# Selective attention and a SwiGLU block on one core: loads of batch 0 and tile 0 in another order and on another queue, narrow score banks, and the first down product by halves

## The chip, the cores and the metric

One core of a Trainium2 chip runs the whole program. TensorE (PE) multiplies, VectorE (DVE), ScalarE (ACT) and GpSimd (POOL) do the rest, SyncE (SP) only issues transfers. The metric is device time in microseconds (us), lower is better, as the median of several runs.

## The reference

Eight batches of eight heads, 576 positions, head size 64, all float32. Causal attention with a bias from the running sum of `max(s, 0)`; its output, as 4608 tokens of 512, goes through a SwiGLU block of width 1536.

```python
scores = scale * np.matmul(q, k.transpose(0, 1, 3, 2))
cum = np.cumsum(np.maximum(s, 0.0), axis=-1)
bias = -(cum[:, :, :, None] - cum[:, :, None, :])
scores = np.where(causal, -1000000000.0, scores + np.minimum(bias, 0.0))
attn = softmax(scores)
x = (attn @ v).transpose(0, 2, 1, 3).reshape(4608, 512)
g = x @ w_gate
out = (g * sigmoid(g) * (x @ w_val)) @ w_out
```

## The kernel before

The order of all work is written out by hand: each engine runs its instructions in the order in which the program emits them, and semaphores hold one engine until another is done. So where a line stands decides what is queued behind it.

**Attention.** Heads are taken in groups of four (`hb`, 0 to 15), k and q of one group being one load each (`load_one`, 576 KB). Before their use they are cast to bfloat16 (`cast_one`, `cast_half`), turned so that the head's dimension lies across partitions, and put into `KQ[hb % 2]`. For groups 0 to 4 TensorE turns them (`pe_transpose`, then `pe_out` copies them out of PSUM, one copy for each pair of heads, `r`); from group 5 (`NPE`) on they go out to DRAM (`scratch`), come back by a DMA transpose (`transposes`) and are copied into place by DVE (`split`, held in the list `later` and emitted by `do_later`). Four more rows of `KQ` hold the bias: running sums and constants from the tile `HL`, sent there by four small transfers a group (`aug`). The product of the 68 used rows gives score and bias together, keys across partitions.

`score_piece(bh, ci)` makes the scores of head `bh` in four pieces: the four diagonal blocks (512 columns), two pieces of 512 columns below them, and the last diagonal block (64). In batch 0 (`pair`) two pieces share a PSUM tile two banks wide, and one exponential takes 1024 or 576 columns; later, each piece has its bank and its exponential. GpSimd then zeroes the upper triangles of the diagonal blocks (`affine_select`, L391 and L396). `av_piece` multiplies with V (`VT`, filled chunk by chunk by `cast_v`), with a column of ones that gives the sum; `av_out` divides. A pair of heads is then turned into `XT`, by TensorE for batches 0 and 1 (`x_pe`), later through DRAM.

**Feed-forward.** Tokens go in nine tiles of 512 (`tt`), which do not begin where batches do. `gate_value` makes 24 items a tile, gate and value products in turn, 12 column blocks (`ft`) of each; weights lie in halves `j` of 768 columns, loaded and cast by GpSimd's transfers (`w_load`). `down_plain` (tiles 0 and 1) multiplies back with `WO`, four blocks of 128 tokens one after the other; `down_seven` does it with seven products for eight in the rest.

**The order.** At the start, `first_batch` emits batch 0 head by head, with loads, casts and transposes between. A second set of eight one-bank PSUM buffers (`take` gives the one released longest ago, `give` hands it back) then takes the place of the first set. After that the main loop walks through the items of each tile; after every item `pump` emits as much attention of the next batch (`attn_items`) as the item's number says. For tile 0 it starts at item `n0`. Between score pieces, `side`, `side_v` and `PREP_AT` emit loads, casts and transposes at fixed places (head, piece). `hook` does so at items of tile 0.

**Queues.** Loads of k, q and V and the transposes are issued on SP; weights, most of `aug` and the stores on GpSimd, whose own work waits while it issues. V's tile has one buffer (`bufs=1`), so that a batch's V is loaded only when the last one's is cast. k and q have three buffers.

Of the kernel before, what the change touches and what calls it, by code (L numbers as in the profile page):

```python
# [19 lines left out]
def kernel(  # L20
# [18 lines left out]
    NCH = 5  # L39
# [67 lines left out]
    PTP = {0: first, "bufs": 8}  # L107

    with tc.manual_schedule():
# [3 lines left out]
        first_psum = ExitStack()  # L113
        psa = first_psum.enter_context(tc.tile_pool(name="psa", bufs=1, space=PSUM))
        bank = {}
        for i in range(2):
            bank["w", i] = psa.tile([128, 1024], FP32, name=f"wide{i}")
        for i in range(4):
            bank["s", i] = psa.tile([128, 512], FP32, name=f"one{i}")
        released = {key: i - 8 for i, key in enumerate(bank)}  # L120
# [3 lines left out]
        def take(kind="s"):  # L124
            b = min((x for x in bank if x[0] == kind), key=lambda x: released[x])
            assert released[b] < OPEN
            released[b] = OPEN
            return b
# [5 lines left out]
        def second_psum():  # L134
            assert all(x < OPEN for x in released.values())
            at_end = dict(released)
            first_psum.close()
            psb = ctx.enter_context(tc.tile_pool(name="psb", bufs=1, space=PSUM))
            bank.clear()
            released.clear()  # L140
            for i in range(8):
                bank["s", i] = psb.tile([128, 512], FP32, name=f"bank{i}")
                released["s", i] = at_end["w", i // 2] if i < 4 else at_end["s", i - 4]

# [6 lines left out]
        def load_one(hb, name, rs=(0, NR)):  # L151
            b, g = divmod(hb, 2)
            if rs[0] == 0:
                loaded[name, hb] = raw.tile([128, NR, J, D], FP32, tag="raw" + name, name="raw" + name)
            nc.sync.dma_start(
                loaded[name, hb][:, rs[0] : rs[1], :, :].rearrange("x r j d -> x r (j d)"),
                SRC[name][0][b, g * HB + 2 * rs[0] : g * HB + 2 * rs[1], :, :].rearrange(
                    "(r e) (p j) d -> (e p) r (j d)", e=2, j=J
                ),
            )  # L160
# [5 lines left out]
        def load_v(b, cs):  # L166
# [3 lines left out]
            for c in cs:  # L170
                n = 128 if c < 4 else TAIL
                nc.sync.dma_start(  # L172
# [13 lines left out]
        NEGS2 = -1.0058441162109375  # L186

# [22 lines left out]
        load_qk(1)  # L210
# [6 lines left out]
        make_identity(nc, ident)  # L217

# [10 lines left out]
        pads(0)  # L229
        init_vt(0)  # L230
        init_vt(1)
        nc.vector.memset(aug_rows(1, 0), 0.0)
        nc.gpsimd.memset(aug_rows(1, 1), 0.0)
# [114 lines left out]
        scs = {}  # L348

        def score_piece(bh, ci):  # L350
            hb, hh = divmod(bh, HB)
            pair = bh < H
            if ci == 0:
                pts[bh] = PTP[0].tile(
                [128, PTW], BF16, tag="pt", bufs=PTP["bufs"], name="pt"
            )
# [3 lines left out]
            if pair:  # L360
                if ci % 2 == 0:
                    bs = take("w")
                    scs[bh] = bs
                else:
                    bs = scs[bh]
                base = (512, 0, 0, 512)[ci]
            else:
                bs = take()
                base = 0
            o = base  # L370
            n = sum(hi - lo for _, lo, hi in CHUNKS[ci])
            sc = view(bs, 1024 if pair else 512)
            for (tj, lo, hi) in CHUNKS[ci]:
# [5 lines left out]
                    start=True,  # L379
                    stop=True,  # L380
                )
                o += w
            if not pair or ci % 2 == 1:
                if pair:
                    c0, W = ((576, 1024), (0, 576))[ci // 2]
                else:
                    c0, W = CHUNK_PT[ci], n
                nc.scalar.activation(pt[:, c0 : c0 + W], sc[:, 0:W], AF.Exp, scale=0.125)  # L388
                give(bs)
            if ci == (1 if pair else 0):  # L390
# [89 lines left out]

        def side(h, step, ci):
            bh = HB * h + step
            if bh == H + 3 and ci == 1:
                for c in range(5):
                    cast_v(1, c, nc.gpsimd)
            if h >= 3 and h + 3 < NHB and (step, ci) == (0, 1):
                load_qk(h + 3)
            hb = h + 1
            if NPE <= hb < NHB:
                late = hb == NPE  # L490
                if (step, ci) == (0, 1):
                    if late:
                        transposes(hb)
                    aug(hb, GP4)
                first = 1 if hb < NPE + 2 else 0
                if step in (first, first + 1) and ci == 1:
# [3 lines left out]
            if NPE <= hb < NHB:  # L500
                late = hb == NPE
                if (step, ci) == ((1, 1) if late else (0, 2)):
                    cast_one(hb, "k", nc.scalar)
                if (step, ci) == ((2, 1) if late else (1, 2)):
                    cast_one(hb, "q", nc.scalar)
                if (step, ci) == ((3, 1) if late else (2, 0)):
                    scratch(hb)
                if (step, ci) == (3, 3 if hb == NPE + 1 else 0) and not late:
# [5 lines left out]
            if 2 <= bn < B:  # L514
# [5 lines left out]

        V_AT = {(1, 0): 0, (2, 0): 1, (2, 2): 2, (3, 0): 3, (3, 2): 4}

        def side_v(h, step, ci):
            bn = h // 2 + 1
            if 2 <= bn < B and h % 2 == 1 and (step, ci) in V_AT:
                cast_v(bn, V_AT[step, ci], nc.scalar if bn > 2 else nc.gpsimd)

        def prep_one(hb, i):
# [3 lines left out]
            for r in range(2):  # L532
                pe_out(hb, nm, g, r, nc.scalar if nm == "k" else nc.vector)

        PREP_AT = {
            2: {(0, 3): 0, (1, 3): 1, (2, 1): 2, (2, 3): 3},
# [5 lines left out]
            H + 5: (H + 2, H + 3), H + 6: (H + 4, H + 5), H + 7: (H + 6,),  # L542
        }
        X_AT = {H + 3: (), H + 5: (H + 1,), H + 6: (H + 3,), H + 7: (H + 5,)}

        def attn_items():
            for kk in range(H, BH + 2):
                h, step = divmod(kk, HB)
                if kk < BH:
# [5 lines left out]
                    if step == 0 and 3 < h + 1 < NPE:  # L555
# [62 lines left out]

        def gate_value(tt, hps, sus):
            xt = XT[:, :, (tt % 3) * TT : (tt % 3 + 1) * TT]  # L620
            for ft in range(NFT):
                j, f0 = divmod(ft * 128, WCH)
                gbs = take()
                pg = view(gbs, TT)
                for c in range(4):
                    nc.tensor.matmul(  # L626
                        pg, WG[j][:, c, f0 : f0 + 128], xt[:, c, :],
                        start=(c == 0), stop=(c == 3),
                    )
# [8 lines left out]
                vbs = take()  # L638
                pv = view(vbs, TT)
                for c in range(4):  # L640
                    nc.tensor.matmul(  # L641
                        pv, WV[j][:, c, f0 : f0 + 128], xt[:, c, :],
                        start=(c == 0), stop=(c == 3),
                    )
# [19 lines left out]
        def down_plain(tt, hps):  # L664
            for ts_ in range(4):
                ybs = take()
                py = view(ybs, DM)
                half, c0 = divmod(ts_ * 128, HT)
                for ft in range(NFT):
                    nc.tensor.matmul(  # L670
                        py, hps[ft // 2][:, 2 * (ft % 2) + half, c0 : c0 + 128],
                        WO[ft // WKO][:, ft % WKO, :],
                        start=(ft == 0), stop=(ft == NFT - 1),
                    )
                    if ft % 4 == 3 and ft < NFT - 1:
                        yield 1.0
                if ts_ % 2 == 0:
                    ysb = yp.tile([128, 2, DM], FP32, tag="y", name="ysb")
                nc.scalar.copy(ysb[:, ts_ % 2, :], py)
                give(ybs)  # L680
# [6 lines left out]
                yield 1.0  # L687
# [166 lines left out]

        cast_half(0, "k", 0, nc.scalar)
        cast_half(0, "q", 0, nc.scalar)
        aug(0, SP4)
        load_v(0, range(5))
        load_qk(2)
        for nm in ("k", "q"):  # L860
            for g in range(2):
                pe_transpose_half(0, nm, g, 0)
        pe_out(0, "k", 0, 0, nc.scalar)
        pe_out(0, "k", 1, 0, nc.scalar)
# [142 lines left out]
```

The softmax here doesn't subtract the row's maximum and nothing guards it: scores larger than these inputs give would overflow.

## Time and profile before

| | |
|---|---|
| median of 4 runs | 380.27 us (380.19 to 380.38) |
| the profiled execution's own time | 380.29 us |
| its span, first to last instruction | 378.5 us |
| busy: PE, DVE, ACT, POOL | 361.7, 291.1, 242.5, 206.3 us |
| DMA, share of 16 engines' span: SP's queue, GpSimd's | 50.0%, 17.9% |
| chain that ended last, largest: PE, SP's queue, DVE, DMA | 81%, 7%, 4%, 3% |
| mean granted TensorE clock | 0.999 |

The profile is of one execution. A busy TensorE is not one at its peak: a matmul of 512 columns is drawn 0.379 us long, while four in a row are 0.86 us apart. Times inside the span count from its first instruction; the profiled run is 1.8 us longer than its span. In a line of the timeline stand start, length, engine, source line, operation, out<-in, shapes and count; in brackets stands the idle time of the engine before it and what ended that. A name such as `SPq` is an engine's queue, which issues and waits. Of PE's 0.379 us only the spacing costs time, and an engine's idle time costs nothing unless someone waits for it.

### The profile page before, as it was taken

Reading aid. Unit: us, or ns where it says so; the run is one execution under the profiler, and the core shown is the slowest. Engines: PE = TensorE matmul, PEld = TensorE weight load, DVE = VectorE, ACT = ScalarE, POOL = GpSimd, SP = SyncE. Lnnn points to the kernel's source line nnn. Section 1 sums busy time; section 2 is a strip of 40 time slices with the busy share of each in tenths; the row PEclk is TensorE's granted clock in tenths of the full one; section 3 lists DMA queues with packets and bytes.
Section 4 is the critical chain, followed back from the end, with each engine's and each line's share of the span. In section 5 each row is a group of like instructions: output and inputs, shape, how many; then the busy total and the mean of one; then the engine's idle time right before and its main releaser. Section 6 shows DMA issues by size and latency. Waiting matters only on the chain.

```text
span 378.5 us, 8674 instructions
## 1 busy us (share of the span) xinstructions
PE 361.7 (96%) x3246; PEld 228.8 (60%) x3246; DVE 291.1 (77%) x577; ACT 242.5 (64%) x459; POOL 206.3 (55%) x326
## 2 busy tenths in 40 slices
PE   3789999999999999999999999999999999999996
PEld 3575545655555555865586558755775575466465
DVE  7776776557895899869975999589958876985984
ACT  7776876787977777578767885697365523323321
POOL 6792347555364646595558656775675426224320
PEclk9999999999999999999999999999999999999999
DMA  7999999997588997498769765897233033001103
GB/s 245 187 250 263 198 217 293 337 280 175 157 165 279 219 286 186 132 292 208 177 201 281 205 161 160 227 205 159 48 70 117 22 30 128 0 2 68 44 2 111
DMA packets 100729, 64.22 MB, mean 170 GB/s; under 512 B 81888, under 2 KB 85824, under 8 KB 100688
## 3 DMA queue, kind: packets, MB, share of 16 engines
q1 hardware_dynamic: 91248, 46.15, 50.0%
q0 software_dynamic: 9440, 17.53, 17.9%
q8 instruction: 25, 0.41, 0.5%
q14 instruction: 16, 0.13, 0.1%
HBM read 37.90 MB, written 19.86 MB: 153 GB/s over the span
## 4 chain that ended last, share of the span: by engine, by line
PE 81%; SPq 7%; DVE 4%; DMA 3%; ACT 2%; issue 1%; POOL 0%; DVEq 0%; ACTq 0%
PE bank L626 21%; PE bank L641 21%; PE bank L711 17%; PE bank L375 9%; SPq L172 7%; PE bank L413 6%; PE bank L670 5%; DMA rawk<-in_k_dram 2%; PE wide L375 2%; ACT pt L388 1%; DVE pp L633 1%; DMA s_sb<-in_s_dram 1%; DMA kq<-HL 1%; PE one L413 1%; DVE ht L649 1%
## 5 line engine op out<-in xcount | busy, mean ns | idle before, releaser
L388 ACT ACTIVATE pt<-bank 128x512 bf16<-128x512 f32 x224 | 106.7, 507 | 25.9 <-PE bank L375 17.6
L626 PE MATMUL bank<-XT,wg 128*128 128x512 bf16 x432 | 110.9, 379 | 0.6 <-DVE pp L633 0.2
L641 PE MATMUL bank<-XT,wv 128*128 128x512 bf16 x432 | 110.9, 379 | 0.0
L631 ACT ACTIVATE th<-bank 128x512 bf16<-128x512 f32 x108 | 64.7, 599 | 59.5 <-PE bank L626 56.4
L633 DVE SCALAR_TENSOR_TENSOR pp<-th,bank 128x512 bf16<-128x512 bf16 x108 | 73.7, 683 | 26.8 <-ACT th L631 26.3
L649 DVE SCALAR_TENSOR_TENSOR ht<-pp,bank 128x512 bf16<-128x512 bf16 x108 | 74.2, 687 | 10.3
L658 POOL TENSOR_TENSOR ht<-ht 128x512 bf16<-128x512 bf16 x35 | 40.4, 1154 | 53.1 <-DVE su L656 53.0
L375 PE MATMUL bank<-kq 128*128 128x128 bf16 (+4 forms) x504 | 67.5, 240 | 0.2 <-DVE ht L649 0.2
L375 PEld LDWEIGHTS <-kq 128*128 128x128 bf16 x576 | 46.3, 98 | 32.6 <-issue 4.8
L626 PEld LDWEIGHTS <-wg 128*128 128x128 bf16 x432 | 38.4, 98 | 35.7 <-issue 1.7
L641 PEld LDWEIGHTS <-wv 128*128 128x128 bf16 x432 | 38.3, 98 | 35.3
L391 POOL TENSOR_SCALAR_AFFINE_SELECT pt<-pt 128x512 bf16<-128x512 bf16 x64 | 41.7, 652 | 27.9 <-ACT pt L388 27.3
L413 PEld LDWEIGHTS <-pt 128*128 128x128 bf16 x960 | 41.1, 98 | 17.4 <-issue 1.6
L413 PE MATMUL bank<-vt,pt 128*128 128x65 bf16 x840 | 42.1, 194 | 1.5 <-POOL vt L183 0.8
L447 POOL DMA_DIRECT2D xs<-ot x24 | 21.7, 906 | 28.2 <-DVE ot L430 28.2
L711 PEld LDWEIGHTS <-ht 128*128 128x128 bf16 x336 | 31.2, 98 | 4.3
L197 POOL DMA_DIRECT2D kq<-HL x52 | 31.6, 610 | 0.1
L430 DVE TENSOR_TENSOR ot<-bank,rc 128x320 bf16<-128x320 f32 x56 | 27.5, 492 | 1.9
L396 POOL TENSOR_SCALAR_AFFINE_SELECT pt<-pt 128x64 bf16<-128x64 bf16 x64 | 17.3, 270 | 18.2 <-ACT pt L388 18.0
L711 PEld LDWEIGHTS <-su 128*128 128x128 bf16 x252 | 23.6, 98 | 3.3
L670 PE MATMUL bank<-wo,ht 128*128 128x512 bf16 x96 | 24.7, 379 | 0.0
L776 POOL TENSOR_TENSOR ysb<-ysb 128x512 f32<-128x512 f32 x12 | 15.2, 1270 | 15.3 <-DVE ysb L770 15.3
(96 smaller groups left out, 395.6 us busy)
## 6 DMA issues: line engine op xcount, KB each, us to landing
rawk<-in_k_dram SPq DMA_DIRECT2D x15, 576.0 KB
rawq<-in_q_dram SPq DMA_DIRECT2D x15, 576.0 KB
rawv<-in_v_dram SPq DMA_DIRECT2D x32, 256.0 KB
out_dram<-ysb POOLq DMA_DIRECT2D x32, 256.0 KB, 3.9
xs<-ot POOLq DMA_DIRECT2D x24, 160.0 KB, 3.8
ks<-ck SPq DMA_DIRECT2D x11, 288.0 KB
qs<-cq SPq DMA_DIRECT2D x11, 288.0 KB
wg<-in_moe_w_gate_dram POOLq DMA_DIRECT2D x2, 768.0 KB, 14.0
```

The costliest lines, as they stand in the source:

```text
L375: nc.tensor.matmul(sc[:, o : o + w], T[:, 1, e * S + 128 * tj : e * S + 128 * (tj + 1)], T[:, 0, e * S + lo : e * S + hi], start=True, sto ...
L388: nc.scalar.activation(pt[:, c0 : c0 + W], sc[:, 0:W], AF.Exp, scale=0.125)
L391: nc.gpsimd.affine_select(pt[:, 1088:1600], pt[:, 1088:1600], pattern=[[0, 4], [1, 128]], compare_op=ALU.is_ge, fill=zreg, base=0, channel ...
L413: nc.tensor.matmul(av[:, bi * (D + 1) : (bi + 1) * (D + 1)], pt[:, c0 : c0 + 128], VT[b % 2][:, tj, h, :], start=(tj == 0), stop=(tj == bi),)
L626: nc.tensor.matmul(pg, WG[j][:, c, f0 : f0 + 128], xt[:, c, :], start=(c == 0), stop=(c == 3),)
L631: nc.scalar.activation(th, pg, AF.Tanh, scale=0.5)
L633: nc.vector.scalar_tensor_tensor(pp, in0=th, scalar=1.0, in1=pg, op0=ALU.add, op1=ALU.mult)
L641: nc.tensor.matmul(pv, WV[j][:, c, f0 : f0 + 128], xt[:, c, :], start=(c == 0), stop=(c == 3),)
L649: nc.vector.scalar_tensor_tensor(hp[:, 2 * k2 : 2 * k2 + 2, :].rearrange("p a n -> p (a n)"), in0=pp, scalar=0.5, in1=pv, op0=ALU.mult, op ...
L658: (nc.vector if ft == NFT - 1 else nc.gpsimd).tensor_sub(hp[:, 1:3, :], hp[:, 1:4:2, :], hp[:, 0:3:2, :])
L670: nc.tensor.matmul(py, hps[ft // 2][:, 2 * (ft % 2) + half, c0 : c0 + 128], WO[ft // WKO][:, ft % WKO, :], start=(ft == 0), stop=(ft == NF ...
L711: nc.tensor.matmul(ps, lhs(p), rhs(p), start=(first and p == 0), stop=(last and p == NP - 1), skip_group_check=True,)
```

## The change

- **Loads.** k and q of group 1, V of batch 0, and k and q of groups 2 and 3 go on GpSimd's queue and no longer on SP's. The first weights come right behind V 0, and the others follow in pieces (`w_load` of halves) between GpSimd's casts of V 0 and of group 2. `wo` is loaded at items 12 and 14 of tile 0. V 1 and k, q of groups 4 and 5 stay on SP, right behind each other.
- **Scores of batch 0** use the eight one-bank buffers from the start, each piece with its own exponential. For the diagonal pieces TensorE first writes a mask (`ident` times `lower`, which holds -32768 above the diagonal) and the scores add to it; GpSimd's selects of batch 0 are gone.
- **Order of batch 0.** It is written out line by line: products with V of heads 0 and 1 stand after the scores of head 4, and so on; three gate products of tile 0 are begun with three of their four parts before the last pair's `x_pe`. TensorE multiplies the identity 32 times at the start and twice ten times later.
- **Group 2's `prep_one`** moves to items 3 to 6, its second copies come at the next item; attention starts at item 7 (`n0`). Group 3 is prepared at other places, group 5 is cast later (head 15), stored at head 16, turned three pieces later. V 1 is cast in steps over heads 11 and 12; V 2 is loaded after head 12 and cast at heads 17 and 18.
- **Tile 0's down product** runs over the first half of `WO` for all four token blocks (four banks open), then over the second.

```diff
-    PTP = {0: first, "bufs": 8}
+    PTP = {0: first, "bufs": 7}
+    lower = first.tile([128, 512], BF16)
...
-        for i in range(2):
-            bank["w", i] = psa.tile([128, 1024], FP32, name=f"wide{i}")
-        for i in range(4):
-            bank["s", i] = psa.tile([128, 512], FP32, name=f"one{i}")
+        bank = {i: psb.tile([128, 512], FP32, name=f"bank{i}") for i in range(8)}
...
-        load_qk(1)
...
+        nc.gpsimd.memset(lower, 0.0)
+        nc.gpsimd.affine_select(
+            lower, lower, pattern=[[0, 4], [1, 128]],
+            compare_op=ALU.is_ge, fill=nc.gpsimd.to_reg(MASKED), base=0, channel_multiplier=-1,
+        )
...
+        for nm in ("k", "q"):
+            load_one(1, nm, eng=nc.gpsimd)
...
+            masked_here = masked and ci in (0, 3)
+            if masked_here:
+                nc.tensor.matmul(
+                    sc, ident, lower[:, 0:n], start=True, stop=False, skip_group_check=True
+                )
...
+        V1_AT = {
+            (H + 3, 3): (0, 1), (H + 4, 0): (2,), (H + 4, 1): (3,), (H + 4, 2): (4,)
+        }
...
-            if bh == H + 3 and ci == 1:
-                for c in range(5):
-                    cast_v(1, c, nc.gpsimd)
...
+            if bh == H + 4 and ci == 3:
+                load_v(2, range(5))
+            if h == 4 and (step, ci) in ((0, 1), (2, 1)):
+                load_qk(6 + step // 2)
...
+                if late and (step, ci) == (0, 1):
+                    scratch(hb)
+                if late and (step, ci) == (0, 3):
+                    transposes(hb)
...
+            order = [(ts_, j) for ts_ in range(4) for j in range(NWCH)]
+            if tt == 0:
+                order.sort(key=lambda x: x[1])
...
+        keep_warm(32)
         cast_half(0, "k", 0, nc.scalar)
         cast_half(0, "q", 0, nc.scalar)
         aug(0, SP4)
...
+        row_half("k", 0, nc.scalar)
+        row_half("q", 0, nc.vector)
+        cast_half(0, "k", 1, nc.scalar)
+        cast_half(0, "q", 1, nc.gpsimd)
+        load_v(0, range(5), nc.gpsimd)
+        w_load("g", 0)
+        nc.gpsimd.memset(aug_rows(1, 1), 0.0)
+        aug(1, SP4)
+        keep_warm(10)
+        row_half("k", 1, nc.scalar)
+        row_half("q", 1, nc.vector)
+        keep_warm(10)
+        cast_one(1, "k", nc.vector)
+        cast_one(1, "q", nc.vector)
+        for c in range(3):
+            cast_v(0, c, nc.gpsimd)
+        w_load("v", 0, 0)
+        for c in range(3, 5):
+            cast_v(0, c, nc.gpsimd)
+        for nm in ("k", "q"):
+            load_one(2, nm, eng=nc.gpsimd)
+        w_load("v", 0, 1)
+        for nm in ("g", "v"):
+            w_load(nm, 1, 0)
+        load_one(3, "k", eng=nc.gpsimd)
+        scores(0)
+        half_batch("k")
+        scores(1)
+        half_batch("q")
+        scores(2)
+        scores(3)
...
+        scores(4)
+        values(0, 1)
+        scores(5)
+        values(2, 3)
+        scores(6)
+        values(4)
+        x_pe(0, nc.vector)
+        scores(7)
+        aug(3, SP4)
+        load_v(1, range(5))
+        load_qk(4)
+        load_qk(5)
+        values(5)
+        x_pe(1, nc.vector)
+        values(6)
+        x_pe(2, nc.scalar)
+        values(7)
+        for ft in range(3):
+            products("g", ft, XT[:, :, 0:TT], range(3))
+            if ft == 0:
+                x_pe(3, nc.scalar)
...
+        for i in range(4):
+            at_item(3 + i, prep_one, 2, i)
+        at_item(10, cast_one, 3, "k", nc.gpsimd)
+        at_item(11, cast_one, 3, "q", nc.gpsimd)
+        at_item(12, w_load, "o", 0)
+        at_item(14, w_load, "o", 1)
...
-            n0 = 6 if tt == 0 else 0
+            n0 = 7 if tt == 0 else 0
...
-                if i >= 2 * NFT or i % 4 == 1:
+                if i >= 2 * NFT or i % (2 if tt == 1 else 4) == 1:
                     do_later(1)
+                while seconds:
+                    seconds.pop(0)()
```

`products(kind, ft, xt, cs)` is the gate or value product of one block over the parts `cs`, and goes on with one that was begun; `row_half` turns one pair of heads of group 0; `half_batch` turns k or q of group 1 and copies out the first pair's half, the second follows after the scores of head 3; `scores` and `values` are four `score_piece`, and `av_piece` with `av_out`.

## The prediction

> **What bounds the kernel now.** I read the page first, to see which engine is full, then the windows of the first 65 us, then the timelines and the chain of waits of that stretch.
>
> ```profile
> PE 361.7 (96%) x3246; PEld 228.8 (60%) x3246; DVE 291.1 (77%) x577; ACT 242.5 (64%) x459; POOL 206.3 (55%) x326
> ...
> PE   3789999999999999999999999999999999999996
> ...
> GB/s 245 187 250 263 198 217 293 337 280 175 157 165 279 219 286 186 132 292 208 177 201 281 205 161 160 227 205 159 48 70 117 22 30 128 0 2 68 44 2 111
> ```
>
> TensorE is full from the fourth slice on. No edit takes work away from it, so time can come only from the first slices and from holes. The windows show how large these are:
>
> ```profile
> 15.00:20.00 5.00, 2.63 (x28) 1.88 (x26) 4.94 (x9) 4.47 (x7) 5.00 (x10) 1.00 1.19 240
> ...
> 35.00:40.00 5.00, 4.59 (x34) 2.51 (x32) 4.69 (x7) 3.64 (x8) 2.52 (x3) 1.00 1.13 243
> ...
> 50.00:55.00 5.00, 4.49 (x35) 2.45 (x34) 3.81 (x6) 3.77 (x9) 1.65 (x4) 1.00 0.87 174
> 55.00:60.00 5.00, 4.70 (x49) 2.68 (x47) 2.47 (x6) 1.79 (x3) 4.93 (x10) 1.00 1.00 383
> 60.00:65.00 5.00, 4.27 (x57) 2.70 (x56) 2.41 (x6) 4.19 (x8) 2.91 (x4) 1.00 1.13 248
> ```
>
> Columns: window, its length, then busy us of PE, PEld, DVE, ACT, POOL, clock, DMA share, GB/s. In 15 to 20 us PE works 2.63 of 5, while ACT (4.47), DVE and POOL are nearly full: batch 0's attention is bound by the exponentials and what feeds them. Of 30 to 65 us PE lacks about 2.2 us (0.2 + 0.4 + 0 + 0.1 + 0.5 + 0.3 + 0.7). The timeline of PE names the holes, those of ACT and the chain what lies behind:
>
> ```profile
> 30.17 1.02 PE L626 MATMUL bank<-XT,wg 128*128 128x512 bf16 x4 [0.17 <-ACT XT L468]
> ...
> 54.70 0.19 PE L413 MATMUL bank<-vt,pt 128*128 128x65 bf16 x1 [0.51 <-POOL vt L183]
> ...
> 56.30 0.65 PE L413 MATMUL bank<-vt,pt 128*128 128x65 bf16 x16 [0.30 <-POOL vt L183]
> ...
> 60.75 0.45 PE L297 MATMUL bank<-ident,ck 128*128 128x128 bf16 x5 [0.52 <-POOL ck L256]
> ```
> ```profile
> 28.45 6.41 SPq L172
> ...
> 34.91 7.53 SPq L172
> ```
> ```profile
> 18.83 6.70 ACT L388 ACTIVATE pt<-wide 128x1024 bf16<-128x1024 f32 x8
> ...
> 37.91 1.69 ACT L388 ACTIVATE pt<-bank 128x512 bf16<-128x512 f32 x4
> ...
> 60.77 1.15 ACT L254 CAST ck<-rawk 128x1152 bf16<-128x1152 f32 x1 [1.88 <-DMA rawk<-in_k_dram]
> ```
> ```profile
> 8.69 0.66 POOL L266 CAST cq<-rawq 128x576 bf16<-128x576 f32 x1 [1.75 <-DMA rawq<-in_q_dram]
> ```
>
> The first feed-forward product starts at 30.17. The holes at 54 to 63 us are late loads: V of batch 1 (SP stood 6 to 7 us at each of its issues) and k of group 5, for which ACT stood 1.88 us.
>
> **Batch 0, step by step.** *Start.* Scores start at 10.82, when the bias rows (kq<-HL) land at 10.78; that chain does not change. But k and q of group 1 leave the SP queue for GpSimd's, where they run beside the last half of q 0 instead of behind it. That half was cast at 8.69; then come 0.66 of cast, 1.0 of nine transposes, and ten new warm matmuls (14 of them took 0.51 + 0.62, so 0.6 for ten): scores at 11.0 if q is undisturbed. GpSimd's first load can move data near 6 us, so 2.7 us of q's load may run at half rate: 0 to 2.6 us later. I take 0.9, a third of it, as most of q 0 is through by then.
>
> *Pace.* Two wide exponentials a head: eight in 6.70, 1.72 a head by their starts in the chain (17.11, 18.83, 20.54). Four narrow ones: 1.69 with the last one's 0.23, of which some 0.1 is its own slot: 1.56 a head. So the split costs ACT nothing, it gives 0.15 a head. The mask now costs PE two matmuls a head, 0.22 + 0.03, times 8 = 2.0 us; it lies in a stretch where PE idles half of its time. POOL loses 8 x (0.63 + 0.24) = 7.0 us. If PE were the bound there, all 2.0 would show.
>
> *New stops, PE being in order.* The transposes of k 1 stand before head 1's scores and need DVE's cast (pe_out of q 0 1.46, then 0.78): 0.65 us of ACT idle. The products of heads 0 and 1 (0.9) stand between the scores of heads 4 and 5: 1.05. Later ones 0.3 and 0.25. Sum 2.2. First exponential at 11.65 (scores + 0.65); 11.65 + 8 x 1.56 + 2.2 = 26.3 for the last, against 25.5 now.
>
> *V 0 on GpSimd.* After the cast of q (9.35) POOL issues five V loads, wg, a memset (1.10), casts three chunks (0.58 each), issues a half wv (0.8), casts two. An issue of V (1,024 runs) is not in the trace: 0.58 (kq<-HL) to 1.45 (xs<-ot, 0.906 for 640 runs, scaled); I take 1.0, nearer to the second by kind, as wo with 768 runs takes 0.83. 9.35 + 5.0 + 0.8 + 1.1 + 1.75 + 0.8 + 1.15 = 19.95. PE comes to those products at 19.4, so this costs about 0.1 more; at 1.45 it is 2.2 more. Against it speaks a row of sharing: DVE's V cast beside POOL's selects took 1.209 us for 512 columns, while its cast of 1,152 columns with POOL idle took 0.782; DVE's two casts of k 1 and q 1 (0.78 + 0.74) lie beside these issues, so 0 to 1.5 later; I take 0.3.
>
> The Trainium skill (SBUF — State Buffer, Who interferes with whom) says more sharply that a DMA issued from GpSimd waits for its descriptors while a VectorE copy holds the shared port, and advises the sync queue there. By it V 0 would be 1.5 us later, and the sum below 1.2 us smaller; no row of this trace shows an issue held up so.
>
> *End.* Today: last exponential 25.5, then products, transposes, copies on ACT, first gate matmul 30.17: 4.6 us. After: products of head 7 and DVE's division 1.5, transposes of pair 3 0.4, then nine gate matmuls of three quarters, of which six (1.3) cover the copy: 26.3 + 3.2 = 29.5, with 9 x 0.215 = 1.9 us of tile 0 done. That equals a start at 27.6, so 2.6 before 30.17; less 0.9 for q and 0.4 for V: **1.3 us gained**, bounds 2.6 and -1.5.
>
> **Tile 0.** Bytes before tile 0 can run: s 0.15, k and q of two groups 2.3, V 1.15, wg 0.77, half of wv 0.38 = 4.8 MB; at 227 GB/s (mean of the first three slices) from 2 us: there by 23 to 24, needed at 29. Up to its down stage: another 7.4 MB (k and q of groups 2 to 4, rest of wv, both second halves, V 1, wo 0); the first six slices moved 12.9 MB by 57 us; needed at 60. So the demand order fits, with 3 us to spare. V 1 is cast from head 11's last piece on, near 53, in steps of 0.6 between POOL's selects. Its load starts near 28 as now, but the k and q of group 3, which stood before it in the same queue, are on GpSimd's, and wo comes later (items 12 and 14): I put its landing at 49 to 50. The casts of group 5 move from heads 13 and 14 to head 15, near 67 us. So these holes go: 0.51 + 0.30 + 0.52 + 0.21 of PE (the last is DVE's wait behind ACT's 1.88) = 1.5, and each restart hides 0.16 more (a 512-wide matmul is drawn 0.379 long and spaced 0.215): 1.5 + 4 x 0.16 = **2.2 us**, bounds 3.2 (all holes go) and 0.
>
> What is late next: tile 0's down by halves holds four of eight banks for six items, while scores, products and group 4's transposes share four. ACT turns a bank over in about 1.1 us and attention needs five in 4 us, so I put it at 0.1. Scratch 5 and its DMA transposes now go out at heads 16, near 71 to 73, behind load_qk(6) on SP; the trace's SP waited up to 4.3 us for such a store, and an issue of pk<-ks takes 1.6, so the k half lands near 81, and DVE meets its first copy out of it near 80. DVE standing 1 us there costs PE 0 to 1.5; I take 0.5. V 2's issues and aug wait on SP alone. Everything else of tile 0 (0.75 steps, one prep half an item later) has the same instructions; the attention's start at item 7 for 6 only shifts work within the tile. Cost 0.6, bounds 0 and 2.5.
>
> **Sum.** The profiled run took 380.29 us for a span of 378.5, and the median is 380.27, so the sum is made against 380.29. -1.3 - 2.2 + 0.6 = -2.9: **377.4 us**. The likeliest case itself spans 375.8 to 379.2.
>
> **Rivals.** *All of it* (chance 0.17): q 0 undisturbed, V 0 in time, no new stop: -2.6 - 3.2 = 374.5. For it: POOL and SP have idle time everywhere in these windows. Against: every second queue named above runs beside another at a DMA share over 1.
>
> *A wash* (0.10): the start gains nothing (q 0 by 2 us late) and holes move from 54 to 63 on to the transposes of group 5: 380.0. The DMA share is over 1 from 15 to 50 us now, and no byte is saved; that speaks for it.
>
> *Slower: GpSimd's queue is the bound* (0.23). GpSimd is in order, and the casts of V 0, the second weights and the loads and casts of group 2 stand behind its five V issues. Price: q at 11.2, cast 11.9, five issues at 1.45, other steps 5.6, 1.5 of DVE in the way: V 0 ready at 26.2 for 19.9, so heads 0 and 1 hold PE and, two heads later, ACT: the start of tile 0 at 27.6 + 6.2 = 33.8, 3.6 late, which the 2.2 of tile 0 do not pay: 381.7. It decides from V 0 ready at 24.2 on, where 2.6 + 2.2 - 0.6 = 4.2 is used up. For it: each of its terms is a row; against: all at their worst at once.
>
> The main case has 0.50. Differences under 0.2% (0.76 us) this kernel's measurement can't tell from none. Faster: 0.50 + 0.17 = 0.67; same 0.10; slower 0.23. The range leaves about 0.2 out: from the full gain, 374.2, to 381.4, most of the slower case.
>
> **What would show it.** Right: in the new profile's timeline the last exponential of batch 0 ends at 26 to 28, narrow ones in groups of 1.56 a head; gate matmuls of three quarters stand before the last XT copy; the first product of V 0 waits for POOL by less than 1 us; no hole of PE from POOL's vt or ck at 50 to 63; ACT's cast of group 5 has no idle before it. Wrong: PE holes at 17 to 24 ended by POOL vt; scores that start after 12.5; a PE hole at 78 to 86 behind DVE's copies out of pk or pq; ACT idle while PE waits for a bank in the down stage.

## The result, and the profile after

The changed kernel takes 378.88 us in the median (378.43 to 382.44), the one before 380.19 (378.82 to 382.62): a ratio of 0.997, interval 0.9961 to 0.9978, so 1.3 us faster where 2.9 were forecast. The profiled execution took 378.65 us with a span of 376.7, against 380.29 with 378.5. Ratios here and below leave out runs more than 1.5% above the fastest of their kernel (seven of the twelve in the experiment e15, none elsewhere).

First the busy time of the engines on the page of after, then the windows of 30 to 65 us (columns as before):

```profile
PE 364.7 (97%) x3300; PEld 231.2 (61%) x3300; DVE 290.9 (77%) x577; ACT 242.8 (64%) x473; POOL 211.2 (56%) x324
```
```profile
35.00:40.00 5.00, 3.65 (x26) 1.94 (x25) 4.33 (x7) 3.10 (x8) 0.76 (x2) 1.00 1.20 239
...
50.00:55.00 5.00, 4.21 (x34) 2.32 (x34) 3.49 (x7) 3.48 (x8) 3.62 (x7) 1.00 1.10 279
55.00:60.00 5.00, 5.00 (x64) 3.29 (x63) 4.23 (x9) 3.40 (x8) 4.12 (x7) 1.00 1.13 301
60.00:65.00 5.00, 5.00 (x66) 3.41 (x65) 3.38 (x7) 3.26 (x7) 2.41 (x5) 1.00 1.17 237
```

From 55 us on TensorE is full, where it lacked 0.3 and 0.7. But 35 to 40 now lacks 1.35 and 50 to 55 lacks 0.8. TensorE's timeline names these holes, and shows the new start:

```profile
26.85 0.81 PE L631 MATMUL bank<-XT,wg 128*128 128x512 bf16 x3
...
29.88 1.03 PE L631 MATMUL bank<-XT,wv 128*128 128x512 bf16 x4
...
37.15 0.82 PE L359 MATMUL bank<-kq 128*128 128x128 bf16 x8 [1.35 <-DVE kq L316]
50.78 0.38 PE L359 MATMUL bank<-kq 128*128 128x128 bf16 x4 [0.88 <-DVE kq L316]
```

At 29.88, when the first value product begins, ten gate matmuls are done, 0.217 each: that equals a start at 27.7, 2.45 sooner than 30.17. Every hole that V 1's or group 5's loads had made is gone. In their place head 8's scores (37.15) wait for VectorE's last copy of group 2's q, and head 12's for group 3's. VectorE's timeline shows why:

```profile
30.71 0.69 DVE L647 SCALAR_TENSOR_TENSOR pp<-th,bank 128x512 bf16<-128x512 bf16 x1 [2.87 <-ACT th L645]
31.50 0.69 DVE L658 SCALAR_TENSOR_TENSOR ht<-pp,bank 128x512 bf16<-128x512 bf16 x1
...
36.40 0.70 DVE L316 COPY kq<-bank 64x512 bf16<-64x512 bf16 x1
37.01 0.66 DVE L647 SCALAR_TENSOR_TENSOR pp<-th,bank 128x512 bf16<-128x512 bf16 x1
```

From its first gate operation on VectorE works without a pause until 39.1, the copies standing among `pp` and `ht`. That operation came 1.2 us sooner than before (31.91), yet the copy that head 8 needs ends at 37.1, as it did in the kernel before. There it is the first of the two at 36.38, and head 8's scores start at 37.21 without a wait (VectorE's row, then TensorE's, both of before):

```profile
36.38 1.46 DVE L326 COPY kq<-bank 64x512 bf16<-64x512 bf16 x2
```
```profile
37.21 0.82 PE L375 MATMUL bank<-kq 128*128 128x128 bf16 x8
```

So the chain has become longer, 6.4 us from the first gate operation to the end of that copy for 5.2 before. Six gate operations stand ahead of the copy where four stood, because the change moved group 2's preparation from items 1 to 4 to items 3 to 6.

To size the terms I took, for each TensorE instruction, the time to the next one's start less the median spacing of its shape. In us, the changed kernel against the one before:

| term | forecast | in the two profiles |
|---|---|---|
| start of batch 0 | -1.3 | -2.45 |
| old holes of tile 0 (50 to 70 us) | -2.2 | -1.9 |
| new stops of tile 0 (30 to 50 us) | +0.6 | +1.8 |
| rest of TensorE's stream | 0 | +0.25 |
| after TensorE's last matmul | not in the sum | +0.5 |
| sum | -2.9 | -1.8 |

The last row but one: TensorE ends at 374.86 in 378.5 before, and at 372.54 in 376.7 after. That is 2.3 us gained, of which the span keeps 1.8.

### The profile page after: what moved, and what is told of

It is laid out like the page before. It is cut to its first block, busy times and chain, and to the rows that moved or that the text cites. A ratio compares the mean times of both kernels' runs of the same rounds, so it can differ in the third digit from the quotient of the medians.

```text
span 376.7 us, 8798 instructions
## 1 busy us (share of the span) xinstructions
PE 364.7 (97%) x3300; PEld 231.2 (61%) x3300; DVE 290.9 (77%) x577; ACT 242.8 (64%) x473; POOL 211.2 (56%) x324
## 4 chain that ended last, share of the span: by engine, by line
PE 86%; DVE 5%; ACT 4%; DMA 3%; issue 1%; DVEq 0%; ACTq 0%
PE bank L631 45%; PE bank L730 16%; PE bank L359 10%; PE bank L396 7%; PE bank L681 5%; DMA pk<-ks 3%; ACT pt L369 1%; DVE kq L316 1%; DVE pp L647 1%; DVE ht L658 1%; PE bank L446 1%; PE bank L287 1%; DVE kq L274 1%; ACT kq L215 1%; PE bank L353 1%
## 5 line engine op out<-in xcount | busy, mean ns | idle before, releaser
L369 ACT ACTIVATE pt<-bank 128x512 bf16<-128x512 f32 (+1 forms) x256 | 120.5, 507 | 31.2 <-PE bank L359 18.0
L359 PE MATMUL bank<-kq 128*128 128x128 bf16 (+4 forms) x576 | 75.0, 240 | 2.9 <-DVE kq L316 2.2
L374 POOL TENSOR_SCALAR_AFFINE_SELECT pt<-pt 128x512 bf16<-128x512 bf16 x56 | 36.7, 655 | 29.9 <-ACT pt L369 29.3
L396 PE MATMUL bank<-vt,pt 128*128 128x65 bf16 x960 | 46.6, 194 | 0.6 <-DVE ot L413 0.5
L430 POOL DMA_DIRECT2D xs<-ot x24 | 21.7, 904 | 30.4 <-DVE ot L413 28.1
L413 DVE TENSOR_TENSOR ot<-bank,rc 128x320 bf16<-128x320 f32 x64 | 31.5, 492 | 2.2
L183 POOL DMA_DIRECT2D kq<-HL x48 | 29.2, 610 | 0.0
L681 PE MATMUL bank<-wo,ht 128*128 128x512 bf16 x96 | 25.9, 379 | 0.0
L730 PEld LDWEIGHTS <-su 128*128 128x128 bf16 x252 | 23.6, 98 | 3.3
L379 POOL TENSOR_SCALAR_AFFINE_SELECT pt<-pt 128x64 bf16<-128x64 bf16 x56 | 15.0, 267 | 17.5 <-ACT pt L369 17.4
```

The costliest lines, as they stand in the source:

```text
L359: nc.tensor.matmul(sc[:, o : o + w], T[:, 1, e * S + 128 * tj : e * S + 128 * (tj + 1)], T[:, 0, e * S + lo : e * S + hi], start=not maske ...
L369: nc.scalar.activation(pt[:, c0 : c0 + n], sc, AF.Exp, scale=0.125)
L374: nc.gpsimd.affine_select(pt[:, 1088:1600], pt[:, 1088:1600], pattern=[[0, 4], [1, 128]], compare_op=ALU.is_ge, fill=zreg, base=0, channel ...
L396: nc.tensor.matmul(av[:, bi * (D + 1) : (bi + 1) * (D + 1)], pt[:, c0 : c0 + 128], VT[b % 2][:, tj, h, :], start=(tj == 0), stop=(tj == bi),)
L413: nc.vector.tensor_mul(ot[:, :, e * D : (e + 1) * D], av3[:, :, 0:D], rc[:, :, None].to_broadcast([128, NCH, D]),)
L681: nc.tensor.matmul(view(pys[ts_], DM), hps[ft // 2][:, 2 * (ft % 2) + half, c0 : c0 + 128], WO[j][:, ft % WKO, :], start=(ft == 0), stop=( ...
```

## The experiments

Holes are TensorE's idle times in its timeline. Unless said, edits are on the changed kernel and times are medians; "before" is the kernel before on the same chip. The runs were on several chips, where the kernel before took 380.0 to 380.5 us, so runs are best compared by their ratios.

**Is the hole at 37 us VectorE's chain, and does order in it matter?** Three runs prepare groups 2 and 3 sooner (e1 puts group 2 back at the items of the kernel before), a fourth leaves out the nine begun gate matmuls.

```diff
# e1: group 2                      (e3 = e1 + e2)
-            at_item(3 + i, prep_one, 2, i)
+            at_item(1 + i, prep_one, 2, i)
# e2: group 3 at (1,0) (1,2) (2,0) (2,2) for (1,2) (2,0) (2,2) (3,0), cast at items 9 and 10
# e4:
-            products("g", ft, XT[:, :, 0:TT], range(3))
```

> The changed kernel with the preparation of group 2 at items 1 to 4 of tile 0 for items 3 to 6, nothing else moved. Theory (head 8's scores wait for DVE's copies of q, which stand behind its products of the first blocks; 1.35 us of idle PE at 37.2 us): that hole goes or falls under 0.4 us and the kernel is 1.0 to 1.5 us faster than the changed one, 377.4 to 377.9 for 378.9. Rival (DVE is full from 30 to 39 us, so copies that come sooner push its products back and PE runs out of banks instead): a hole of the same size elsewhere before 45 us, time within 0.4 us of 378.9.

> The changed kernel with the four preparations of group 3 each one place sooner (heads 9.0, 9.2, 10.0 and 10.2 for 9.2, 10.0, 10.2 and 11.0) and the two casts ahead of them one item sooner. Theory (head 12's scores wait 0.88 us at 50.8 for the last of DVE's copies of q): that hole goes, 0.8 to 1.0 us faster than the changed kernel, 377.9 to 378.1, hole at 37 us unchanged. Rival (the queue of ACT and DVE around 46 to 52 us is what PE waits for, whichever copy is last in it): same time as the changed kernel within 0.4 us.

> Both moves: group 2 prepared at items 1 to 4 and group 3 one place sooner. Theory: the two holes are apart and add up, 2.0 to 2.5 us faster than the changed kernel, 376.4 to 376.9; no hole of PE over 0.5 us between 28 and 70 us. Rival (one shortage of DVE moves from place to place): the sum is less than either alone would say, 377.8 to 378.9, with a new hole before 60 us.

> The changed kernel without the nine gate matmuls that are begun ahead of the last x_pe copy (the blocks are then made whole in tile 0's items, as they were before). Theory (PE's head start of 1.9 us is given back at head 8's scores, because DVE starts no sooner for it): the hole at 37 us shrinks from 1.35 us to under 0.5 us, and the time stays within 0.5 us of 378.9. Rival (what PE does early is time gained): 1.5 to 1.9 us slower, 380.4 to 380.8, hole at 37 us unchanged.

e1 took 378.24 (ratio 0.9945, 0.9925 to 0.9965), e2 378.65 (0.9955), e3 378.07 (0.9947, 0.9928 to 0.9966), e4 379.01 (0.9972, 0.9952 to 0.9992). e1 leaves 0.34 + 0.21 of the first hole's 1.35, where the kernel before had 0.20 + 0.21 (39.41 and 40.01), and the second as it was; e2 leaves the first and turns the second into 0.31 + 0.34 at 46 to 47. e2's time is within 0.4 us of the changed kernel's, as its rival had it. In e3 the two holes have broken up into four, behind other operations of the same engine:

```profile
37.91 0.38 PE L359 MATMUL bank<-kq 128*128 128x128 bf16 x4 [0.34 <-DVE ht L658]
38.50 1.02 PE L631 MATMUL bank<-XT,wv 128*128 128x512 bf16 x4 [0.21 <-DVE pp L647]
...
46.31 0.38 PE L359 MATMUL bank<-kq 128*128 128x128 bf16 x4 [0.31 <-DVE kq L316]
47.03 1.02 PE L631 MATMUL bank<-XT,wv 128*128 128x512 bf16 x4 [0.34 <-DVE ht L658]
```

Their 1.2 us for 2.23 is the gain (0.8 us against 378.88): the first hole was made by the change's own order, and what stays is VectorE's amount of work. In e4 the first hole shrank to 0.57 and the time did not change: what the begun matmuls had won was lost again behind VectorE.

**The kernel before, once more.** 

> The kernel before, unchanged, for a second profile: from the last matmul's end to the span's end it takes 3.6 us in the first profile, the changed kernel 4.2. Theory (the landing of the last stores differs from execution to execution): 3.6 to 4.3 us. Rival (something in the change makes the end longer): 3.6 again within 0.1 us. The holes of PE at 54.7, 56.3, 60.8 and 63.2 us come again with 0.2 to 0.6 us each.

380.02 us in the median. In this execution tile 0 began 1.9 us later than in the profile shown, and the holes at 54 to 63 us were absent; TensorE ended at 374.57, as early as ever. That fits loads that set the end of tile 0, with a "start" and "holes" that were not two separate sums, as a later start fed on the holes; it is one execution. From TensorE's last matmul to the end of the span it took 3.6 us again, for 4.15 after, so the longer end belongs to the change.

**Taking work off VectorE; V 1's steps; down by halves.**

```diff
# e5 = e3 and
-            seconds.append(lambda: pe_out(hb, nm, g, 1, eng))
+            seconds.append(lambda: pe_out(hb, nm, g, 1, nc.scalar if hb < 4 else eng))
# e6: V 1 cast in a row
-            (H + 3, 3): (0, 1), (H + 4, 0): (2,), (H + 4, 1): (3,), (H + 4, 2): (4,)
+            (H + 3, 1): (0, 1, 2, 3, 4)
# e7: tile 0's down in the old order
-            if tt == 0:
-                order.sort(key=lambda x: x[1])
```

> Group 2 at items 1 to 4 and group 3 one place sooner, and besides the second copies of q (0.7 to 0.8 us each, four of them) go from DVE to ACT. Theory as it stands now (the head start of PE is lost because DVE is full from 31 to 41 us and again near 46; the copies are the part of its work that can go): the remaining holes (0.34 and 0.21 us at 38 us, 0.31 and 0.34 at 46 to 47) fall to under 0.3 in sum, 0.5 to 1.0 us faster than with the two moves alone, 377.1 to 377.6. Rival (ACT, which stands at its exponentials and tanh there, becomes the late one): holes of the same sum, released by ACT, 377.9 to 378.5.

> The changed kernel with all five casts of V 1 back at head 11's second piece in a row, as they stood before. Theory (the order of the loads, not the place of the casts, took away the holes at 54 and 56 us: V 1 has landed by 45 us): no hole behind POOL's vt, time within 0.4 us of 378.9. Rival (the steps are needed): the two holes come back, 0.8 to 1.2 us slower than the changed kernel, 379.7 to 380.1.

> The changed kernel with tile 0's down product in the order of before, one block of tokens after the other. Theory (it was there for a late second half of wo; wo 0 lands near 53 us and wo 1 near 61): the second half is wanted from about 62 us on instead of 68, so a hole of 0 to 0.8 us behind wo and a time of 378.9 to 379.6. Rival (four open banks cost PE waits that the order of before does not have): 0.2 to 0.6 us faster, 378.3 to 378.7.

e5 took 378.67 (0.996, 0.9939 to 0.9981), no better than e3. Its holes at 37 to 47 are gone, but TensorE, now earlier, meets V 1's stepped casts:

```profile
54.31 0.28 PE L396 MATMUL bank<-vt,pt 128*128 128x65 bf16 x4 [0.89 <-POOL vt L168]
54.87 0.19 PE L396 MATMUL bank<-vt,pt 128*128 128x65 bf16 x1 [0.28 <-POOL vt L168]
```

e6 took 379.04 (0.9991, 0.9956 to 1.0025; two runs at 383.62 and 384.06 widen it) and shows both VectorE holes and none behind `vt`: it was the order of the loads that removed V 1's old holes, not the steps. e7 took 378.86 (0.9973, 0.9951 to 0.9994) without a hole behind `wo`: the down by halves is worth nothing here that this measurement can tell.

**All three together, and the end of the kernel.** e8 is e5 with e6's row of casts. e9 is e8 with one transfer fewer on SP; e12 is the changed kernel with that edit alone.

```diff
-        aug(3, SP4)
+        aug(3, [nc.sync] * 3 + [nc.gpsimd])
```

> Groups 2 and 3 prepared sooner (items 1 to 4; one place sooner with casts at items 9 and 10), their second q copies on ScalarE, V 1 cast in one row at head 11 piece 1. Theory: what ate the forecast is a chain of DVE places (q copies of groups 2 and 3, then tanh and product of the gate), plus, once these are gone, V 1's stepped casts; with all three taken away no hole of TensorE over 0.4 us stays between 30 and 60 us, and the 1.2 us of holes that were left at 37 to 47 with both groups sooner come off 378.07: 376.8 to 377.6. Rival (PE is held by what feeds the attention in total, a hole closed here opens there): 378.0 to 378.8, with a new hole of 0.5 us or more between 45 and 65 us.

> The same with one of SP's transfers (the last bias row of group 3) on GpSimd, so that SP's count of transfers is one lower and the last store falls on the semaphore that SP waits for last. Theory (after the last landing SP goes through seven more waits of 0.06 us): the stretch from the last matmul's end to the span's end falls from 4.0-4.2 to 3.6-3.7 us, and the time lies 0.4 us under the run without it: 376.4 to 377.2. Rival (the tail's length is set by the store itself): 4.0 to 4.2 and no difference.

> The changed kernel with only the last bias row of group 3 on GpSimd, so that SP has one transfer fewer. Theory: the two holes behind VectorE at 37 and 51 us stay (1.3 and 0.9), the stretch from TensorE's last matmul to the span's end falls from 4.0-4.2 to 3.6-3.7, time 378.2 to 378.7 (0.4 less than 378.88). Rival: no part of the end depends on which semaphore is waited for last: 378.9.

| run | median (range) | ratio | TensorE's end, span |
|---|---|---|---|
| e8 | 377.85 (376.44 to 381.84) | 0.9943 (0.9911 to 0.9975) | 371.24, 375.3 |
| e9 | 376.49 (376.24 to 378.19) | 0.989 (0.9855 to 0.9926) | 371.23, 374.9 |
| e12 | 378.34 (377.77 to 378.55) | 0.9951 (0.9934 to 0.9968) | 372.94, 376.7 |

In e8 and e9 TensorE has no hole over 0.3 us between 30 and 66 us. In e9's windows:

```profile
35.00:40.00 5.00, 4.76 (x31) 2.42 (x30) 3.43 (x6) 4.90 (x11) 1.62 (x2) 1.00 1.18 263
...
50.00:55.00 5.00, 5.00 (x56) 3.04 (x55) 3.52 (x6) 4.20 (x10) 4.17 (x9) 1.00 1.13 294
```

VectorE has fallen from 4.33 to 3.43 of 5 us in the first, ScalarE has risen from 3.10 to 4.90. e8's median lies 0.25 above what its theory gave, its profiled run (377.33) inside. As for the end, the last store in after (span 376.7), then in e9 (span 374.9):

```profile
373.26 0.40 SPq L829 DMA_DIRECT2D out_dram<-ysb  x1
```
```profile
371.95 0.41 SPq L829 DMA_DIRECT2D out_dram<-ysb  x1
```

From the issue of that store to the end are 3.4 us after and 2.9 in e9; before it was 2.9 (375.58 of 378.5). SP's own rows show what differs. At the end it waits for nine semaphores in turn, 0.06 us each when the event is there. In after the second wait ends 1.44 before the span's end and seven more follow; in e9, as before, the wait that ends last (0.90 before the end) is the ninth. One transfer more or fewer on SP decides on which place the last store falls. From TensorE's last matmul to the end are 4.15 us after, 4.05 in e8, 3.62 in e9 and 3.71 in e12, so the edit is worth about 0.4. In the medians e12 is 0.54 below the changed kernel, with intervals that overlap, and e9 is 1.36 below e8, of which the rest is the spread of e8's runs.

**Which part made the start?** e11 puts k and q of group 1 and V 0 back on SP in their old places; e13 does that and puts group 1's bias rows on GpSimd, as before, clear of V 0.

```diff
-            load_one(1, nm, eng=nc.gpsimd)
+            load_one(1, nm)
...
+        load_v(0, range(5))           # behind aug(0, SP4)
-        load_v(0, range(5), nc.gpsimd)
...
-        aug(1, SP4)                   # e13 only
+        aug(1, GP4)
```

> The changed kernel with k and q of group 1 and V of batch 0 on SP's queue, in the places of before. Theory (the queue of the first loads moves only the start, and the start is given back behind DVE at 37 us): the half of q 0 is cast at 8.5 to 8.9 for 7.86, the first exponential within 0.5 us of 11.4, V 0's casts before 19; the first gate matmul 26.5 to 27.5; time 378.6 to 379.3, the same as the changed kernel's. Rival (the queue move is what made the start 2.4 us earlier): first gate matmul at 28.5 or later, time 379.5 or more.

> The changed kernel with k and q of group 1 and V of batch 0 on SP, as before, and the bias rows of group 1 on GpSimd, as before, so that they do not stand behind V 0's issues. Theory (an issue of V 0 takes 1.6 us on SP and 0.97 on GpSimd, so V 0 comes later there): V 0's casts done at 22 to 23 instead of 18.96, the products of heads 0 and 1, due at 19.4, hold TensorE for 2 to 3 us, first gate matmul at 28.5 to 30, time 380.3 to 382. Rival (the loads are bound by what the memory delivers, whichever queue issues them): V 0 cast by 19.5, time 378.6 to 379.2.

Both are slower than before: e11 384.18 (1.0086, 1.0055 to 1.0117), e13 384.90 (1.0124, 1.0103 to 1.0145). SP's queue, then TensorE's timeline, in e13:

```profile
10.52 8.83 SPq L157 DMA_DIRECT2D rawv<-in_v_dram  x5
```
```profile
19.18 0.22 PE L396 MATMUL bank<-vt,pt 128*128 128x65 bf16 x2 [0.26 <-POOL vt L168]
20.55 0.25 PE L396 MATMUL bank<-vt,pt 128*128 128x65 bf16 x3 [1.15 <-POOL vt L168]
21.76 0.38 PE L396 MATMUL bank<-vt,pt 128*128 128x65 bf16 x4 [0.96 <-POOL vt L168]
23.14 1.59 PE L396 MATMUL bank<-vt,pt 128*128 128x65 bf16 x21 [1.00 <-POOL vt L168]
...
33.50 0.81 PE L631 MATMUL bank<-XT,wg 128*128 128x512 bf16 x3
```

V 0's five issues take 8.83 us on SP, one of them 3.72; on GpSimd they took 4.84. V 0 is cast at 23.6 for 18.96, and TensorE stands 3.4 us in four holes with little work between. In the windows of 16 to 30 us (columns: length, TensorE's busy time, granted clock, DMA share, GB/s) a second price shows:

```profile
19.00:22.00 3.00, 0.71 (x9) 0.96 0.95 154
22.00:24.00 2.00, 0.89 (x15) 0.50 0.54 33
24.00:26.00 2.00, 2.00 (x22) 0.50 1.18 182
26.00:28.00 2.00, 2.00 (x35) 0.50 1.02 340
28.00:30.00 2.00, 2.00 (x35) 0.86 1.11 330
```

After this stop TensorE runs at half its clock for some 6 us, with eight score matmuls drawn 1.48 for 0.82. This was not in my expectation of 2 to 3 us: tile 0 begins 6.65 later. The Trainium skill (TensorE: Matmul & The Clock Gate, Part 1) has the clock fall to half after one idle window of about 3.4 us. Here it fell sooner: none of e13's four holes is over 1.15 us, and in e11, where TensorE stood from 18.16 to 22.17, the clock is 0.97 in the window of 20.0 to 20.3 us and 0.50 in the next. In e11 the bias rows behind V 0 hold TensorE for 4.01 us, and heads after it run slowly too. In the changed kernel nearly all of such a delay reaches the time (6.65 us of start, 6.0 of time), as it did not in the kernel before. Both holes behind VectorE are there again in e13, the second with 0.87:

```profile
43.80 0.82 PE L359 MATMUL bank<-kq 128*128 128x128 bf16 x8 [1.35 <-DVE kq L316]
```

With a start 6.65 us later they have kept their size, so they come from the order inside tile 0 and not from an early start.

But e13 also lets the first weights out at 9.0 us, beside V 0, where on one queue they stood behind it. e15 is e13 with these behind V 0's first cast:

```diff
-        w_load("g", 0)                # ahead of the memset of aug_rows(1, 1)
...
+        cast_v(0, 0, nc.gpsimd)
+        w_load("g", 0)
+        for c in range(1, 3):
```

> The run with V 0 and k, q of group 1 on SP and the bias rows on GpSimd, but the first gate weights issued only behind the first cast of V 0 (near 16 us for 9.0). Theory A (the order of the bytes decides, not the queue): V 0's five issues take 4 to 5 us on SP as they did in the kernel before (4.35), V 0 is cast at 18 to 20, no TensorE hole behind vt over 0.5 us, first gate matmul at 27 to 29, time 378.5 to 380. Theory B (SP's queue itself is slow where GpSimd's is not): 8 us of issues again, V 0 cast after 22, time 383 or more.

Five of its runs lie between 378.44 and 383.49, seven between 384.41 and 386.67 (median of all 384.54; ratio of the five 1.0026, 0.9982 to 1.0069), so it settles only half. The five issues take 5.00 us again: A is right that SP's queue is not slow by itself. But in the profiled execution (385.73) V 0's last piece, issued at 14.15, lands only at 24.1, beside the weights out at 14.31:

```profile
24.81 1.04 PE L396 MATMUL bank<-vt,pt 128*128 128x65 bf16 x16 [4.98 <-POOL vt L168]
```

with the clock at 0.50 again from 24 to 28. What was shown: V 0 has to be whole by about 20 us, and where its last cast ended 4.7 (e13) and 5.8 us (e15) later than in after, TensorE lost its clock as well. On GpSimd's queue, with the weights behind it, it was in time in each profile. That the bytes which go out beside it decide this is argued, not shown: two of e15's runs, with the same order, took 378.44 and 379.36. Why that last piece took 10 us stays open.

**Warm matmuls and begun products, on e9.** e10 has 1 warm matmul at the start for 32; e14 leaves out the begun products as e4 did.

> The mended kernel (both groups sooner, q copies on ScalarE, V 1 in one row, one SP transfer fewer) with 1 warm matmul at the start for 32. Theory: the nine transposes are drawn near 1.17 us again for 0.67, but the scores of head 0 wait for the bias rows anyway (0.7 to 1.5 us of idle there), so the start moves by 0 to 0.3 and the time by as much: 376.4 to 376.9. Rival (the early clock is what brings the start forward): the first exponential 0.6 us or more later, 377.1 or more.

> The mended kernel without the nine begun gate matmuls. Theory: in the changed kernel they were worth nothing, since what they gained was lost again in the hole behind VectorE; with that hole gone they are worth what they cover, 0.8 to 1.3 us: 377.2 to 377.8. Rival (VectorE still paces tile 0, without a visible hole): the same as the mended kernel, 376.3 to 376.8.

e10 took 376.49 (0.9909, 0.989 to 0.9928): the early nine transposes are drawn 1.17 us again for 0.67, and nothing is lost, as in e9 the scores then wait 1.46 us for the bias rows (they start at 11.61 there and at 11.87 here). e14 took 376.93 (0.9935, 0.9909 to 0.9962; 376.25 to 381.69), its profiled run 376.44 for e9's 376.66, with TensorE's end at 371.01 for 371.23. The median lies between my theory's and the rival's, with a wide spread; the profile speaks against the theory that begun products would pay 0.8 to 1.3 once the hole was gone: from 30 to 40 us the time over the usual spacings is about 0 there and 0.55 with them, so VectorE and ScalarE still pace that stretch without a hole of any size.

## Why the prediction was wrong

The side and the mechanisms of the two gains were right; the sum failed at its third term, and at one that it lacked.

- *New stops, +0.6: +1.8.* This is the step that failed: "Everything else of tile 0 (0.75 steps, one prep half an item later) has the same instructions; the attention's start at item 7 for 6 only shifts work within the tile". The same instructions cost 2.56 us of TensorE's time at two places (idle 1.35 + 0.88 and the restarts; 0.8 of the kernel before's own small stops in 30 to 50 us went), because the change had put them in another order. Group 2's preparation, two items later, left its copy behind two gate operations more, and the begun products brought TensorE there sooner: with the old items (e1) 0.34 + 0.21 stay of the 1.35, without the begun products (e4) 0.57. I read 4.69 of 5 us for VectorE in the windows of before, at 35 to 40 us, and used it nowhere; neither group 2's move nor group 3's did I price. e3, e5 and e8 closed these holes step by step. The terms that I did price were not due: VectorE stood 1.48 us at `pk` (76.49) and TensorE lost nothing; no bank was lacking.
- *Start, -1.3: -2.45.* q 0 was undisturbed by the loads beside it (its half cast at 7.86, before 8.69), so the 0.9 was not paid, and V 0 was ready at 18.96 for my 19.95. The pace was worse than worked out, 1.76 us a head for 1.56 (ScalarE's 20 in 8.82): the exponential of 64 columns takes 0.25 and some 0.08 of idle follow it, where I had put 0.1. The new stops were smaller, 0.4 for 2.2. These two errors, 1.6 and 1.8 us over eight heads, cancelled by luck, so that the last exponential ended at 25.85 for 26.3.

```profile
11.39 8.82 ACT L369 ACTIVATE pt<-bank 128x512 bf16<-128x512 f32 x20 [1.36 <-PE bank L359]
```

- *Old holes, -2.2: -1.9.* All went: V 1's through the loads' order (e6), as it had landed by 46.6 us for the 49 to 50 forecast. Group 5's went with its later cast, which no run took back alone.
- *The end, +0.5.* The sum stopped at TensorE's last matmul. Moving loads from SP shifted the place of the last store among SP's final waits; e9 and e12 give it back.
- *The rival on GpSimd's queue* had its chain right (V 0 late, then TensorE, then ScalarE) and the queue wrong: GpSimd's brought V 0 in time, and SP's, in e13, gave V 0 at 23.6 and tile 0 at 33.5, near the 33.8 of that case, though part of it was the halved clock, which that case did not have. The Trainium skill (SBUF — State Buffer, Who interferes with whom), which I had set beside it, lets a VectorE copy or cast hold off the descriptors of a GpSimd load, or the other way round, whoever comes first, and recommends the other path. The runs show both directions, and their price is small:

```profile
L157 POOL DMA_DIRECT2D rawv<-in_v_dram x5: 839/882/1357, 8.5 to 12.5; - x5
```
```profile
10.67 1.32 DVE L246 CAST ck<-rawk 128x1152 bf16<-128x1152 f32 x1
11.92 1.11 DVE L246 CAST cq<-rawq 128x1152 bf16<-128x1152 f32 x1
```

Columns of the first: least, median and longest issue in ns. One of the five was held 0.48 us, VectorE's two casts took 0.56 and 0.36 more than in e13 (0.76, 0.75), where V 0 was SP's and GpSimd issued only small bias rows beside them; in e9 no issue was held and a cast took 2.00. TensorE waited 0.20 for the cast. My sentence by that page, V 0 1.5 us later, was three times too much, and e13 and e15 show no gain from the queue that it recommends.

## What to carry to other kernels

When a change moves work, follow it to the next engine that is full and count what then stands ahead of it there. On VectorE, already at 4.69 of 5 us, two gate operations ahead of a copy made a hole of 1.35 us in TensorE: "same instructions, only shifted" is a price to be worked out, not a zero. Closing one hole moves the bound to the next late thing (q copies, then the gate's operations, then V 1's casts): test the edits together as well as alone, since e5 by itself looked worthless and with e6 and the end it made e9, 376.49 us (ratio 0.989), faster than both kernels. When the number of transfers on a queue changes, look at the stretch behind the last matmul too.

## What the runs showed of the hardware

- At the end of the program SP waits for its semaphores one by one, 0.06 us each; seven of these behind the last landing made 0.4 to 0.5 us.
- Five issues of V 0 took 4.84 us on GpSimd, 4.35 on SP before, 8.83 on SP with the first weights out beside them, and 5.00 on SP with these behind V 0's first cast.
- In the three profiles where TensorE stood 3.4 to 5 us near 20 us, its granted clock was then 0.50 for 6.8 us (e13: from 21.7 to 28.6), so that a late load at the start was paid for nearly twice (3.4 us of holes, 6.65 of start).
- Exponentials of 512 columns are no cheaper a head than wide ones: 1.76 us for four (three of 512 and one of 64, with 0.08 of idle), where two wide ones took 1.72.
